# x^T k in column halves, relu on ScalarE for early k, mixing transposes behind the tokens', twelve z2 statistics on ScalarE

## Chip, cores and metric

The kernel runs on one core of one Trainium2 chip. The metric is the device time of one execution in microseconds (us): 251.74 us before, the median of three runs (251.51 to 251.84). A profiled execution took 250.06 us, of which 248.3 us lie between its first and its last instruction (the span). The granted TensorE clock was 0.999 of full speed.

## The reference

S = 2048 tokens, D = 512, all in bf16. A linear-attention block with 32 heads of 16 columns is followed by a gMLP block with F = 1792, Fh = 896:

```
h  = x + A(layernorm(x))
h2 = h + B(layernorm(h))

A(x): q, k, v = split(x @ wqkv)
      phi(t) = where(t > 0, t + 1, exp(t)) + 1e-06
      kv = einsum('bhsd,bhse->bhde', phi(k), v);  z = einsum('bhsd->bhd', phi(k))
      num = einsum('bhqd,bhde->bhqe', phi(q), kv)
      den = einsum('bhqd,bhd->bhq', phi(q), z)[..., None] + 1e-06
      return (num / den) @ wo
B(x): z = gelu(x @ w_in);  z1 = z[..., :Fh];  z2 = layernorm(z[..., Fh:])
      g = einsum('ts,bsf->btf', w_sp, z2) + b_sp[None, :, None]
      return (z1 * g) @ w_out
```

## The kernel before

Tokens are cut into 16 tiles of 128 (8 pairs, 4 groups of 512). Everything stays in SBUF (the on-chip working memory); PSUM, where TensorE writes, has 8 banks of 512 fp32 columns for each of 128 partitions. Five engines work side by side, each through its own instructions in order: TensorE (PE) multiplies, VectorE (DVE) and ScalarE (ACT) work element by element, GpSimd (POOL) does small vectors and issues some loads, SyncE (SP) issues most DMAs.

The stages:

1. Tiles of x are loaded and normalised. Statistics are on VectorE (`stats`, `aggr`, L610 and L614), the reciprocal root is Ln and Exp on ScalarE (L624, L626), and the scaling is on VectorE (L638) or, from tile 4 on for three tiles of each four, on ScalarE (L665).
2. Normalised tiles are transposed: tiles 0 to 3 by TensorE with a copy by ScalarE (L690, L695), the others by DMA transposes that SyncE issues (L679), one for each tile. L557 issues another kind of DMA transpose, for the mixing weights w_sp: 64 in all, 16 for each group of 512 output tokens (`wsp0` to `wsp3`).
3. The k projection of a token pair (`k_proj`, eight matmuls, L722) fills two PSUM banks, and so does the q projection of 512 tokens and 256 columns (`q_proj`, eight matmuls, L752). `phi` empties them: ScalarE takes Exp (L701) into an exp buffer `e`, VectorE takes the minimum with 1 (L702), and then the maximum of that and the PSUM tile plus 1 (L709). v is never formed. Instead x^T phi(k) is summed over all 16 tiles in four PSUM banks (`acc`, L739, four matmuls of 512 columns a tile); while it is open, two pairs of banks are left for k and q tiles.
4. x^T phi(k) is copied to SBUF in two row halves (L795 ScalarE, L797 VectorE), multiplied by w_v (L803), masked to the heads (L807), multiplied by w_o (L818) and copied (L823, L826) to give M. Column sums of phi(k) (L770, L774, L778, L787) give the denominators (`den`: L838, then Ln and Exp, L842 and L845), which are spread to all columns (L855 with copies L861, or L877) and scale phi(q) (L881).
5. For each unit of one or two tiles: h = x + phi(q) M (L910, L915), statistics, normalise to `hn` (L638; root on POOL, L631 and L633, but for the first tiles), transpose to `hT` (by TensorE for tiles 0 and 1, by DMA from SyncE's queue for the others).
6. z2 (L938, Gelu L947) by token tiles, with its layer norm, and z1 (L983, Gelu L988), transposed. The statistics of a z2 tile are two `bn_stats` and an aggregate on VectorE (L962) or, where `by_act` says so, a sum from the Gelu itself, a mean on POOL (L952), a Square with a sum on ScalarE (L954) and a division on POOL (L957).
7. Mixing: 16 matmuls for each of 28 tiles (L1013), bias and product on VectorE (L1019, L1022), then the output projection (L1031), the residual (L1037) and the store.

The order of each engine's queue is not that of the text. A planner (`Program.schedule`) runs before the instructions are emitted: each operation has an estimated cost, a priority and its dependencies, and the planner picks for each engine the operation that can start and has the lowest priority value. A list of numbers, `NUDGE`, one for each operation, is added to the priorities. So a change of a cost, of a priority or of the list moves instructions in all queues, and PSUM banks and buffers are handed out in the planned order. Semaphore waits follow from the planned order and the data.

Of the kernel before, what the change touches and what calls it, by code (L numbers as in the profile page):

```python
# [6 lines left out]
BF16 = mybir.dt.bfloat16  # L7
ACT = mybir.ActivationFunctionType
ALU = mybir.AluOpType
# [100 lines left out]
class Program:  # L110
# [294 lines left out]
def bass_sequential_preLN__linear_attn_block__mixer_gmlp__prompt_kernel(  # L405
# [41 lines left out]
    s_eb = Store(nc, "e", 3 * 2 * GW * 2)  # L447
# [55 lines left out]
    eb_v = View(s_eb, 0, [3, 2 * GW], BF16)  # L503
    EB = Pool(3, lambda s, w: eb_v.ap[:, s, :])
# [16 lines left out]
    def bank(i):  # L521
        return lambda a: a[:, i, :]

# [8 lines left out]
    def act_c(n, ps=True, ptr=0):  # L532
        return 0.15 + 0.00085 * n + 0.09 * ptr
# [20 lines left out]
    def load_wsp(tg, sts, after=()):  # L554
        for st in sts:
            dst = wsp[tg][st, :]
            op("sp", 1.3, lambda e, dst=dst, st=st: e.dma_start_transpose(  # L557
                dst.ap(), B_w_sp[tg * GW:(tg + 1) * GW, st * P:(st + 1) * P]),
               w=[dst], dma=(f"wsp{tg}", True), nbytes=-3 * P * GW * 2, prio=5000, after=after)

    load_wsp(0, range(NT))
    load_wsp(1, range(WSP1))


# [40 lines left out]
    op("pe", WARM * 2 * MM, spin, r=[warm], w=[acc()], prio=-9)  # L605
# [500 lines left out]
```

## Time and profile before

| what | number |
|---|---|
| median of three runs | 251.74 us |
| the profiled execution | 250.06 us |
| its span | 248.3 us |
| TensorE granted clock | 0.999 |
| TensorE busy, 0 to 10 / 10 to 20 us | 10.0 us long each: 6.74 / 8.08 |
| TensorE busy, 20 to 30 / 30 to 40 / 40 to 50 us | 9.64 / 9.71 / 9.66 |
| TensorE busy, 50 to 62 us | 10.70 of 12.00 |
| TensorE busy, 142 to 200 us | 57.74 of 58.00 |
| x^T k matmuls, L739 | 379 ns each with their drain, 64 of them issued |
| Exp in phi, L701 | 16 of 1025 ns |
| final of phi, L709 | 16 of 1223 ns |
| z2 statistics on ScalarE, L954 | 8 of 1042 ns, and 195 ns to read each sum |
| DMA transposes of w_sp, L557 | 2.8 us from issue to landing |

How to read it: the span is the time from the first to the last instruction on the chip; the profiled execution is one execution, so its time and the median differ. "Busy" is the time in which an engine has an instruction running. Matmuls overlap, so the mean duration of one (379 ns for 512 columns) is longer than the distance between two. A line number is that of the listing above; a helper's line (L610, L638, L690, L695, L679, L557) stands for several stages.

### The profile page before, as it was taken

To read this page: it belongs to the slowest core of one execution; us is meant where nothing else is said; L and a number is where in the kernel's file an instruction comes from. 1 tells how busy PE (TensorE), PEld (TensorE's weight loads), DVE (VectorE), ACT (ScalarE), POOL (GpSimd) and SP (SyncE) were. 2 spreads that over 40 slices of the span, in tenths; PEclk is the share of its full clock that TensorE was granted. 3 is DMA by queue.
4 is the path that set the end of the run, shared out by engine and by line. 5 is a ranking of instruction groups with operands and counts; after the bars stand their busy time and mean duration, and the time that the engine had idled before them with its cause. 6 is when DMAs were issued, how large, how long until landed. Compare 5 with 4: busy or idle time off the path is not lost.

```text
span 248.3 us, 2993 instructions
## 1 busy us (share of the span) xinstructions
PE 236.6 (95%) x1146; PEld 108.0 (43%) x1168; DVE 135.8 (55%) x256; ACT 81.9 (33%) x117; POOL 25.7 (10%) x66
## 2 busy tenths in 40 slices
PE   5699999997999999999999999999999999999995
PEld 1343444443444445454444444444444444444442
DVE  4997866559989999870233223343322523322443
ACT  3666674359944847978600300000000000000000
POOL 7100010110023332610200000000000000000000
PEclk9999999999999999999999999999999999999999
DMA  7985547899320340444744474111000110000022
GB/s 221 345 173 105 89 97 178 208 238 272 88 45 15 70 84 3 85 91 99 97 98 106 102 91 104 23 42 45 0 0 0 42 45 0 0 0 3 0 84 84
DMA packets 55870, 21.57 MB, mean 87 GB/s; under 512 B 49488, under 2 KB 55120, under 8 KB 55856
## 3 DMA queue, kind: packets, MB, share of 16 engines
q1 hardware_dynamic: 54928, 17.84, 32.6%
q0 software_dynamic: 656, 3.28, 4.2%
q10 hardware_dynamic: 272, 0.26, 0.3%
q8 instruction: 9, 0.15, 0.2%
q14 instruction: 5, 0.04, 0.1%
HBM read 7.47 MB, written 2.10 MB: 39 GB/s over the span
## 4 chain that ended last, share of the span: by engine, by line
PE 84%; DVE 6%; DMA 5%; ACT 2%; SPq 1%; issue 1%
PE ps L1013 39%; PE ps L983 10%; PE ps L938 10%; PE ps L1031 10%; PE ps L910 5%; PE ps L722 4%; PE ps L739 3%; DMA xT_pq_z<-pk_xn_z 3%; PE ps L752 2%; DMA xh<-in_A_x_dram 2%; DVE small L610 2%; ACT e L701 2%; DVE xT_pq_z L709 1%; DVE xT_pq_z L881 1%; SPq L540 1%
## 5 line engine op out<-in xcount | busy, mean ns | idle before, releaser
L1013 PE MATMUL ps<-wsp,pk_xn_z 128*128 128x512 bf16 x328 | 72.9, 379 | 0.4
L1019 DVE TENSOR_TENSOR r<-ps,e 128x512 bf16<-128x512 f32 x28 | 19.4, 692 | 68.2 <-PE ps L1013 68.2
L1013 PEld LDWEIGHTS ps<-wsp,pk_xn_z 128*128 128x128 bf16 x336 | 32.9, 98 | 39.6
L938 PE MATMUL ps<-win,hT 128*128 128x384 bf16 (+1 forms) x124 | 25.8, 352 | 0.6 <-issue 0.4
L983 PE MATMUL ps<-hT,win 128*128 128x512 bf16 x110 | 25.5, 379 | 0.1
L1031 PE MATMUL ps<-wout,xT_pq_z 128*128 128x512 bf16 x111 | 24.6, 379 | 0.1
L1013 PE MATMUL ps<-wqkv_wsp,pk_xn_z 128*128 128x512 bf16 x110 | 24.2, 379 | 0.1
L610 DVE BATCH_NORM_STATS2 small<-xh 128x6 f32<-128x512 bf16 x32 | 21.4, 677 | 3.8 <-DMA xh<-in_A_x_dram 3.5
L701 ACT ACTIVATE e<-ps 128x1024 bf16<-128x1024 f32 x16 | 16.4, 1025 | 18.7 <-PE ps L752 10.9
L988 ACT ACTIVATE xT_pq_z<-ps 128x1024 bf16<-128x1024 f32 x14 | 14.1, 1020 | 19.6 <-PE ps L983 19.5
L947 ACT ACTIVATE pk_xn_z<-ps 128x896 bf16<-128x896 f32 x16 | 14.6, 917 | 13.3 <-PE ps L938 12.6
L938 PEld LDWEIGHTS ps<-win,hT 128*128 128x128 bf16 x128 | 12.5, 98 | 13.1 <-DVE xh L915 0.7
L1037 DVE TENSOR_TENSOR r<-ps,xh 128x512 bf16<-128x512 f32 x16 | 11.1, 692 | 11.7 <-PE ps L1031 11.7
L1031 PEld LDWEIGHTS ps<-wout,xT_pq_z 128*128 128x128 bf16 x112 | 11.0, 98 | 13.2
L1013 PEld LDWEIGHTS ps<-wqkv_wsp,pk_xn_z 128*128 128x128 bf16 x112 | 10.9, 98 | 13.2
L722 PE MATMUL ps<-wqkv_wsp,xT_pq_z 128*128 128x512 bf16 x64 | 15.3, 379 | 1.4 <-DMA xT_pq_z<-pk_xn_z 1.4
L752 PE MATMUL ps<-xT_pq_z,wqkv_wsp 128*128 128x512 bf16 x64 | 15.1, 379 | 1.3 <-ACT xT_pq_z L695 1.3
L983 PEld LDWEIGHTS ps<-hT,win 128*128 128x128 bf16 x112 | 10.9, 98 | 12.6 <-DVE hn L638 0.2
L910 PE MATMUL ps<-pk_xn_z,xT_pq_z 128*128 128x512 bf16 x64 | 15.1, 379 | 0.4 <-DVE xh L915 0.3
L739 PE MATMUL ps<-pk_xn_z 128*128 128x512 bf16 x60 | 14.9, 379 | 0.2
L638 DVE TENSOR_SCALAR pk_xn_z<-pk_xn_z,small 128x896 bf16<-128x896 bf16 x16 | 7.3, 507 | 10.5 <-POOL small L633 10.5
L1022 DVE TENSOR_TENSOR xT_pq_z<-xT_pq_z,r 128x512 bf16<-128x512 bf16 x28 | 11.9, 425 | 1.0
(81 smaller groups left out, 182.0 us busy)
## 6 DMA issues: line engine op xcount, KB each, us to landing
out_dram<-r SPq DMA_DIRECT2D x16, 128.0 KB, 1.7
xh<-in_A_x_dram SPq DMA_DIRECT2D x7, 256.0 KB, 4.9
win<-in_B_w_in_dram POOLq DMA_DIRECT2D x1, 1792.0 KB, 8.2
wqkv_wsp<-in_A_wqkv_dram SPq DMA_DIRECT2D x2, 512.0 KB, 6.6
wout<-in_B_w_out_dram POOLq DMA_DIRECT2D x1, 896.0 KB, 6.6
wsp<-in_B_w_sp_dram SPq DMA_TRANSPOSE x48, 2.8
wqkv_wsp<-in_A_wo_dram POOLq DMA_DIRECT2D x1, 512.0 KB, 4.5
e<-in_B_b_sp_dram SPq DMA_DIRECT2D x1, 512.0 KB, 4.4
```

Source lines behind the costliest of these rows:

```text
L610: op("dve", dve_c(512), lambda e: e.bn_stats(s6.ap(), src.ap()), r=[src], w=[s6], prio=prio)
L701: op("act", act_c(1024), lambda e: e.activation(e_().ap(), t(flat).ap(), ACT.Exp), r=[t()], w=[e_()], prio=prio)
L722: i = e.matmul(t(bank(ti)).ap(), lhsT=lhs.ap()[:, c, :], rhs=rhs.ap()[:, c, :], start=(c == 0), stop=(c == KD - 1))
L739: i = e.matmul(acc(bank(c)).ap(), lhsT=l.ap()[:, c * P:(c + 1) * P], rhs=r_.ap(), start=(n == 0), stop=(n == NT - 1))
L752: r_ = e.matmul(t(bank(i)).ap(), lhsT=lhs.ap()[:, c, :], rhs=rhs.ap()[:, c, :], start=(c == 0), stop=(c == KD - 1))
L910: i = e.matmul(t(bank(ti)).ap(), lhsT=l.ap()[:, c, :], rhs=mw[c, :].ap(), start=(c == 0), stop=(c == KD - 1))
L938: k = e.matmul(t(bank(i)).ap()[:, 0:b - a], lhsT=l.ap()[:, c, :], rhs=win[c, a:b].ap(), start=(c == 0), stop=(c == KD - 1))
L947: op("act", act_c(FH, ptr=by_act), lambda e, t=t, d=d, acc={"accum_out": m.ap()} if by_act else {}: e.activation(d.ap(), t(flat).ap()[:, 0 ...
L983: k = e.matmul(t(bank(i)).ap(), lhsT=l.ap()[:, c, :], rhs=r_.ap()[:, c, :], start=(c == 0), stop=(c == KD - 1))
L1013: k = e.matmul(t(bank(0)).ap(), lhsT=l.ap()[:, s - a, :], rhs=r_.ap()[:, s - a, :], start=(s == 0), stop=(s == NT - 1))
L1019: op("dve", dve_c(512), lambda e: e.tensor_tensor(gb().ap(), t(bank(0)).ap(), bsp().ap()[:, tg * GW:(tg + 1) * GW], ALU.add), r=[t(), bsp( ...
L1031: k = e.matmul(t(bank(0)).ap(), lhsT=l.ap()[:, fc, :], rhs=wout[fc, :].ap(), start=(fc == 0), stop=(fc == KF - 1))
```

## The change

Eight things are changed together.

- **x^T k in halves.** Each tile's product is made of eight matmuls of 256 columns (`HW`) instead of four of 512. The four banks of `acc` are laid out anew: banks 0 and 1 hold the first 256 columns of phi(k) for all four row blocks, banks 2 and 3 the other 256. From pair `AS` = 5 on, the two halves are separate operations. The first matmul no longer opens the sum with `start`: the eight warm-up matmuls on zeros (`spin`), which all went to bank 0, go round the four banks, and the last four leave the sums open.
- **What follows x^T k** is split the same way: each half is copied by its own engine, multiplied by w_v (eight matmuls), and masked (256 columns).
- **Relu by ScalarE** for the k tiles of pairs 0 and 1 (`FR` = 2): `phi` copies relu(t) to a second exp buffer, and VectorE ends with a `tensor_tensor` add of two SBUF tiles in place of the `scalar_tensor_tensor` on PSUM. There are four exp buffers in place of three.
- **The mixing transposes** that SyncE issues early: five of `wsp0` ahead of the first token transposes (`WSP0` = 5); the other eleven and eight of `wsp1` (`WSP1`, was ten) wait until the token transposes have been issued.
- **z2 statistics:** `ZD` = 1 instead of 2, so 12 tiles of 16 take them on ScalarE instead of 8.
- Two of the planner's costs (1.3 to 1.31 for DMA transposes of one tile, and 0.76 for a normalise on ScalarE).
- A new list `NUDGE`, for the new number of operations. By it the order in all queues differs: among others, the statistics of tiles 0 and 1 are aggregated one by one, tiles 2 and 3 are transposed one by one, three q tiles and the column sums stand between the last halves of x^T k, w_in is loaded ahead of w_out, and the denominators of group 3 stand ahead of those of groups 1 and 2.
- `NA` = 1 is unchanged; `N0` = 4 only names a number that stood in the code.

```diff
-    WSP1 = 10
-    DB, DC, SPP, PK, ZD = 6, 7, 8, 0.3, 2
+    AS, FR, FQ, N0, WSP0 = 5, 2, 0, 4, 5
+    WSP1 = 8
+    DB, DC, SPP, PK, ZD = 6, 7, 8, 0.3, 1
...
+    def half(tile, h, fn=None):
+        o = tile(fn)
+        o.keys = [tile.keys[0] + (i,) for i in ((0, 1) if h is None else (h,))]
+        return o
...
-    load_wsp(0, range(NT))
-    load_wsp(1, range(WSP1))
+    load_wsp(0, range(WSP0))
...
+    HW = GW // 2
+    def xk(h, c):
+        return lambda v: v[:, 2 * h + c // 2, c % 2 * HW:(c % 2 + 1) * HW]
     def spin(e):
-        for _ in range(WARM):
-            i = e.matmul(acc(bank(0)).ap(), lhsT=warm.ap()[:, 0:P], rhs=warm.ap(), start=True, stop=True)
+        for w in range(WARM):
+            i = e.matmul(acc(bank(w % KD)).ap(), lhsT=warm.ap()[:, 0:P], rhs=warm.ap(), start=True, stop=w < WARM - KD)
         return i
...
-    def phi(t, dst, prio, two=False):
+    def phi(t, dst, prio, two=False, relu=False):
         e_ = Tile(EB)
         op("act", act_c(1024), lambda e: e.activation(e_().ap(), t(flat).ap(), ACT.Exp), r=[t()], w=[e_()], prio=prio)
+        if relu:
+            u = Tile(EB)
+            op("act", act_c(1024), lambda e: e.activation(u().ap(), t(flat).ap(), ACT.Relu), r=[t()], w=[u()], prio=prio)
...
+            if relu:
+                return e.tensor_tensor(d, a, b, ALU.add)
+            return e.scalar_tensor_tensor(d, a, 1.0 + EPS_PHI, b, op0=ALU.add, op1=ALU.max)
...
-        for n in (2 * p, 2 * p + 1):
-            l, r_ = xn[n, :], pk[n, :]
-            def mm(e, n=n, l=l, r_=r_):
-                for c in range(KD):
-                    i = e.matmul(acc(bank(c)).ap(), lhsT=l.ap()[:, c * P:(c + 1) * P], rhs=r_.ap(), start=(n == 0),
-                                 stop=(n == NT - 1))
-                return i
-            op("pe", 4 * MM, mm, r=[l, r_], w=[acc()], prio=10 * p + KA)
+        for h in ((None,) if p < AS else (0, 1)):
+            for n in (2 * p, 2 * p + 1):
+                hs = (0, 1) if h is None else (h,)
+                l, r_ = xn[n, :], pk[n, hs[0] * HW:(hs[-1] + 1) * HW]
+                def mm(e, n=n, l=l, hs=hs):
+                    for g_ in hs:
+                        for c in range(KD):
+                            i = e.matmul(acc(xk(g_, c)).ap(), lhsT=l.ap()[:, c * P:(c + 1) * P],
+                                         rhs=pk.ap[:, n, g_ * HW:(g_ + 1) * HW], start=False,
+                                         stop=(n == NT - 1 and c % 2 == 1))
+                    return i
+                op("pe", 2 * MM * len(hs), mm, r=[l, r_], w=[half(acc, h)], prio=10 * p + KA + 9 * (h or 0))
...
+    load_wsp(0, range(WSP0, NT), by_dma_ops)
+    load_wsp(1, range(WSP1), by_dma_ops)
...
+    kvmT = [Tile(XN), Tile(XN)]
     for h in range(2):
-        d = xtk[2 * h:2 * h + 2, :]
-        s = acc(lambda v, h=h: v[:, 2 * h:2 * h + 2, :])
+        a, z = h * GW // 2, (h + 1) * GW // 2
+        d = xtk[:, a:z]
+        s = half(acc, h, lambda v, h=h: v[:, 2 * h:2 * h + 2, :].rearrange("p b (t f) -> p (b t) f", t=2))
...
+        vk, m = Tile(PS), kvmT[h]
+        def mm(e, h=h, vk=vk):
+            for i in range(2):
+                c = 2 * h + i
+                for j in range(KD):
+                    k = e.matmul(vk(bank(0)).ap()[:, i * P:(i + 1) * P], lhsT=wv.ap[:, j, c * P:(c + 1) * P],
+                                 rhs=xtk.ap[:, j, c * P:(c + 1) * P], start=(j == 0), stop=(j == KD - 1))
+            return k
+        op("pe", 8 * 0.058, mm, r=[wv.all(), d], w=[vk()], prio=Q0 + 2)
+        op("dve", 0.4, lambda e, vk=vk, m=m: e.tensor_tensor(
+            m().ap()[:, 0:2 * P].rearrange("p (c f) -> p c f", c=2),
+            vk(bank(0)).ap()[:, 0:2 * P].rearrange("p (c f) -> p c f", c=2),
+            bmask.ap.rearrange("p (a f) -> p a f", a=1).to_broadcast([P, 2, P]), ALU.mult),
+           r=[vk(), bmask.all()], w=[m()], prio=Q0 + 2)
```

In the changed program L764 is the line of the x^T k matmuls, L719 that of relu, L744 and L778 those of the k and q projections, L826 and L828 the copies of the halves.

More of the change, by code (lines that the diff above doesn't have):

```diff
@@ L652, in bass_sequential_preLN__linear_attn_block__mixer_gmlp__prompt_kernel @@
         rstd_of(st_x[grp[0]:grp[-1] + 1, 7], rs.all(), pr)
-        by_act = [n for n in grp if n >= 4 and n % 4 >= NA]
+        by_act = [n for n in grp if n % 4 >= NA and n >= N0]
         if by_act:
@@ L697, in transpose_pair @@
                r=[t()], w=[d], prio=prio + 1)
-    def phi(t, dst, prio, two=False):
+    def phi(t, dst, prio, two=False, relu=False):
         e_ = Tile(EB)
         op("act", act_c(1024), lambda e: e.activation(e_().ap(), t(flat).ap(), ACT.Exp), r=[t()], w=[e_()], prio=prio)
+        if relu:
+            u = Tile(EB)
+            op("act", act_c(1024), lambda e: e.activation(u().ap(), t(flat).ap(), ACT.Relu), r=[t()], w=[u()], prio=prio)
         op("dve", 0.12 + 0.27, lambda e: e.tensor_scalar(e_().ap(), e_().ap(), 1.0, EPS_PHI, op0=ALU.min, op1=ALU.add),
            r=[e_()], w=[e_()], prio=prio)
+        x_ = u if relu else t
         def fin(e):
-            a, b = t(None if two else flat).ap(), e_().ap()
+            a, b = (u() if relu else t(None if two else flat)).ap(), e_().ap()
             if two:
                 b = b.rearrange("p (a b) -> p a b", a=2)
-            return e.scalar_tensor_tensor(dst.ap() if two else flat(dst.ap()), a, 1.0 + EPS_PHI, b, op0=ALU.add,
-                                          op1=ALU.max)
-        return op("dve", dve_c(1024), fin, r=[t(), e_()], w=[dst], prio=prio)
+                a = a.rearrange("p (a b) -> p a b", a=2) if relu else a
+            d = dst.ap() if two else flat(dst.ap())
+            if relu:
+                return e.tensor_tensor(d, a, b, ALU.add)
+            return e.scalar_tensor_tensor(d, a, 1.0 + EPS_PHI, b, op0=ALU.add, op1=ALU.max)
+        return op("dve", dve_c(1024, mode=2 if relu else 1), fin, r=[x_(), e_()], w=[dst], prio=prio)
     def k_proj(p, wt, prio):
@@ L730, in bass_sequential_preLN__linear_attn_block__mixer_gmlp__prompt_kernel @@
         t = k_proj(p, wk, 10 * p)
[L731 removed]
+        o = phi(t, pk[2 * p:2 * p + 2, :], 10 * p, relu=p < FR)
         if p == 6:
             load("pool", "win", win.all(), B_w_in.rearrange("(c p) f -> p c f", p=P), D * F * 2, after=[o])
[L734 to L742 removed]
+        for h in ((None,) if p < AS else (0, 1)):
[10 more added lines that the diff above has]
+                op("pe", 2 * MM * len(hs), mm, r=[l, r_], w=[half(acc, h)], prio=10 * p + KA + 9 * (h or 0))
     def q_proj(gq, f, prio):
@@ L755, in q_proj @@
             op("pe", 4 * MM, mm, r=[lhs, rhs], w=[t()], prio=prio)
-        return phi(t, pqT[f:f + 2, gq * GW:(gq + 1) * GW], prio, two=True)
+        return phi(t, pqT[f:f + 2, gq * GW:(gq + 1) * GW], prio, two=True, relu=gq < FQ)
+    load_wsp(0, range(WSP0, NT), by_dma_ops)
+    load_wsp(1, range(WSP1), by_dma_ops)
     Q0 = 10 * NP
@@ L797, in bass_sequential_preLN__linear_attn_block__mixer_gmlp__prompt_kernel @@
             op("dve", dve_c(1024), lambda e, d=d, s=s: e.tensor_copy(d.ap(), s.ap()), r=[s], w=[d], prio=Q0 + 2)
-    vk, kvmT = Tile(PS), Tile(XN)
-    def mm(e):
-        for c in range(KD):
-            for j in range(KD):
-                i = e.matmul(vk(bank(0)).ap()[:, c * P:(c + 1) * P], lhsT=wv.ap[:, j, c * P:(c + 1) * P],
-                             rhs=xtk.ap[:, j, c * P:(c + 1) * P], start=(j == 0), stop=(j == KD - 1))
-        return i
-    op("pe", 16 * 0.058, mm, r=[wv.all(), xtk.all()], w=[vk()], prio=Q0 + 2)
-    op("dve", dve_c(512), lambda e: e.tensor_tensor(
-        kvmT().ap().rearrange("p (c f) -> p c f", c=KD), vk(bank(0)).ap().rearrange("p (c f) -> p c f", c=KD),
-        bmask.ap.rearrange("p (a f) -> p a f", a=1).to_broadcast([P, KD, P]), ALU.mult),
-       r=[vk(), bmask.all()], w=[kvmT()], prio=Q0 + 2)
+        vk, m = Tile(PS), kvmT[h]
[12 more added lines that the diff above has]
+           r=[vk(), bmask.all()], w=[m()], prio=Q0 + 2)
     for b in range(2):
@@ L818, in bass_sequential_preLN__linear_attn_block__mixer_gmlp__prompt_kernel @@
             op("pe", MM, lambda e, t=t, i=i, c=c, r_=r_: e.matmul(
-                t(bank(i)).ap(), lhsT=kvmT().ap()[:, c * P:(c + 1) * P], rhs=r_.ap(), start=True, stop=True),
-               r=[kvmT(), r_], w=[t()], prio=Q0 + 3.5)
+                t(bank(i)).ap(), lhsT=kvmT[c // 2]().ap()[:, c % 2 * P:(c % 2 + 1) * P], rhs=r_.ap(), start=True,
+                stop=True), r=[kvmT[c // 2](), r_], w=[t()], prio=Q0 + 3.5)
         d = mw[2 * b:2 * b + 2, :]
```

15 lines of the change are left out of this document (7 added, 8 removed), and 57 rows, old and new, of the table NUDGE.

## The prediction

> **What bounds the kernel now.** I read the first part of the page (busy time), then the chain that ended last, then TensorE's timeline over the first 62 us, then SyncE's queue over the same stretch, and last the busy times by stage.
>
> ```profile
> span 248.3 us, 2993 instructions
> PE 236.6 (95%) x1146; PEld 108.0 (43%) x1168; DVE 135.8 (55%) x256; ACT 81.9 (33%) x117; POOL 25.7 (10%) x66
> ...
> PE 84%; DVE 6%; DMA 5%; ACT 2%; SPq 1%; issue 1%
> ```
>
> TensorE carries the span; a gain must come out of its idle time. In the chain, from 61.23 us to 245.40 us it never leaves TensorE but for "issue" pieces of 0.05 us and one of 0.41 us. So nearly all the idle time lies before 61.23 us. TensorE's timeline (start, busy, what, idle before):
>
> ```profile
> 14.79 1.89 PE L739 MATMUL ps<-pk_xn_z 128*128 128x512 bf16 x7
> 16.52 1.89 PE L752 MATMUL ps<-xT_pq_z,wqkv_wsp 128*128 128x512 bf16 x8
> 19.00 1.02 PE L722 MATMUL ps<-wqkv_wsp,xT_pq_z 128*128 128x512 bf16 x4 [0.59 <-DMA xT_pq_z<-pk_xn_z]
> 20.23 1.04 PE L722 MATMUL ps<-wqkv_wsp,xT_pq_z 128*128 128x512 bf16 x4 [0.20 <-DMA xT_pq_z<-pk_xn_z]
> ...
> 30.24 1.89 PE L722 MATMUL ps<-wqkv_wsp,xT_pq_z 128*128 128x512 bf16 x8 [0.34 <-DMA xT_pq_z<-pk_xn_z]
> ...
> 41.04 1.89 PE L722 MATMUL ps<-wqkv_wsp,xT_pq_z 128*128 128x512 bf16 x8 [0.28 <-DMA xT_pq_z<-pk_xn_z]
> ...
> 52.47 1.90 PE L752 MATMUL ps<-xT_pq_z,wqkv_wsp 128*128 128x512 bf16 x8
> 54.21 0.24 PE L778 MATMUL ps<-small,hn 128*128 128x2 bf16 x4
> ...
> 61.23 1.04 PE L910 MATMUL ps<-pk_xn_z,xT_pq_z 128*128 128x512 bf16 x4 [0.30 <-DVE xh L915]
> ```
>
> Eight 512-column matmuls start 1.73 us after the eight before (14.79, 16.52), 0.216 us each; the 1.89 shown includes the drain. Counted by starts, k tile 4 stands 0.75 us late (16.52 + 1.73 = 18.25, start 19.00), tile 5 0.37, the fifth k pair 0.50, the seventh 0.44. All four wait for a DMA transpose of normalised x. Why they are late is in SyncE's queue:
>
> ```profile
> 7.29 9.01 SPq L557 DMA_TRANSPOSE wsp<-in_B_w_sp_dram  x6
> 16.34 5.19 SPq L679 DMA_TRANSPOSE xT_pq_z<-pk_xn_z  x4
> 21.57 4.69 SPq L557 DMA_TRANSPOSE wsp<-in_B_w_sp_dram  x3
> 26.31 5.19 SPq L679 DMA_TRANSPOSE xT_pq_z<-pk_xn_z  x4
> 31.55 5.18 SPq L557 DMA_TRANSPOSE wsp<-in_B_w_sp_dram  x4
> ```
>
> Token tile 4 was normalised by 13.3 us (VectorE, L638, 12.87 for 0.40) but issued at 16.34, behind six mixing-weight transposes of 1.50 us each (9.01 / 6).
>
> **The change, part by part.** The order of each queue is that of the changed program.
>
> *Mixing transposes behind the tokens'.* Five instead of six stand before tile 4, none between the token groups; 12 follow tile 15, then the bias load, 7 more, then the h transposes. Tile 4 is issued at 7.29 + 5 x 1.50 = 14.8 and, with the old 2.66 us from issue to use (16.34 to 19.00), usable at 17.5. Tile 5, one 1.30 us issue later, at 18.73, where it was 20.23: 1.50 us. For the others I walked the queues. Tile 9 is ready when ScalarE has normalised it (about 22.0), tile 8 when VectorE has (about 23.4); landing 2.6 later at 24.7 and 26.1, they are due at 28.2. Tiles 12 to 15 land by 37.9 and are due from 36.9 on, the last at 39.9. So the 0.50 and 0.44 go too. Sum: 2.44.
>
> Does something else stop TensorE first? Each q or k tile fills two of four free banks, and its phi must empty them. Rows of one k tile: last matmul issued by 24.56, Exp 24.75 to 25.78, min/add 25.81, final at 26.27 for 1.22, banks free 2.95 us after the tile. The tile after next starts two blocks later, 3.46 us. In the new order this spacing holds at every tile, with 0.4 to 0.5 us of slack, as before. I count 0.
>
> *LayerNorm statistics one by one.* Tile 0's transposes can start at about 5.0 instead of 6.12, but then TensorE waits for tile 5 anyway: 0.
>
> *x^T k in halves.* 64 matmuls of 512 columns become 128 of 256, with 64 more weight loads. No such stream is in the trace. Bounds: 512 columns take 0.216, 384 take 0.162 (L938, 1.51 for four of each), 128 take 0.055 (L690, four in 0.22) to 0.059 (L803, 16 in 0.94), every one with its own load. 256 then take 0.108 to 0.113: 128 of them 13.8 to 14.4 against 13.8. I take 13.8, as the loads (98 ns) fit inside 108, and keep +0.6. The Trainium skill (TensorE: Matmul & The Clock Gate, Back-to-back issue gap) says that in a stream of load and matmul pairs the load counts too, some 81 ns at 128 columns instead of 56; an estimate by that, 25 ns on each of 128, would add 3.2 us. L803's 59 ns disagrees with it.
>
> What the halves gain: the last half's sum ends the stretch, with the three last q tiles and the column sums before it. The old stretch ended with q at 54.21. The new one ends at T = 54.21 - 2.44 - 0.09 (a gap at 51.40 that the new order fills) = 51.68. From there the way to the continuous stream is again a VectorE queue: final of the last q phi (it started when its Exp was done) to T + 1.15, zc 0.15, masked halves 0.4 each around 0.6 of waiting for ScalarE's half copy and eight matmuls, 0.8 until the M matmuls are done, cast 1.15, three scalings 0.6 + 1.15 + 0.6: T + 7.0 to 7.3. Before, 61.23 - 54.21 = 7.02. Cost 0.2; the halves save a wait, but the same VectorE casts and scalings stand behind it. Bounds: -1.0 (if half of the 2.15 us idle there goes: 7.02 less matmuls of 4.87: L778 0.1, L803 0.94, L838 0.98, L818 0.86, L877 0.87, four of L910 0.86, L855 0.25) to +0.6.
>
> *Tile 0 of h.* Its first z2 matmul now follows a second spread and a y pair. Residual add, statistics, Ln, Exp, normalise, transpose, copy (0.69 + 0.70 + 0.18 + 0.5 + 0.4 + 0.4 + 0.6) run through queues with four more spread copies of 1.02 on ScalarE; I find 1.07 us of TensorE idle there, where before has 0.1 + 0.41: cost 0.5. Bounds 0 and 1.
>
> *Relu.* Two more PSUM passes on ScalarE at about 10 and 16 us. Relu isn't in the trace; Exp of that shape is 1.025, Copy 1.019. VectorE saves 2 x (1.22 - 0.68), the second being L881's all-SBUF form. Hidden behind TensorE's wait for tile 5; without that cover 2 us on ScalarE delay two phis by 1. I take 0.
>
> *Twelve statistics on ScalarE.* Four tiles move: ScalarE + 4 x (1.04 + 0.20 + 0.20) = 5.8, POOL + 4 x (0.26 + 0.37), VectorE - 4 x (0.67 + 0.55 + 0.21) = 5.7. The stages:
>
> ```profile
> 62.00:82.00 20.00, 19.49 (x104) 9.17 (x103) 18.99 (x38) 11.63 (x20) 3.77 (x8) 1.00 0.23 53
> 82.00:102.00 20.00, 19.90 (x103) 9.91 (x102) 18.78 (x45) 14.89 (x23) 7.77 (x17) 1.00 0.24 49
> 102.00:122.00 20.00, 19.89 (x97) 9.39 (x97) 8.62 (x22) 15.99 (x25) 5.76 (x13) 1.00 0.54 100
> ```
>
> Columns after the length: PE, PEld, DVE, ACT, POOL. ScalarE has 17.5 us idle here, VectorE 2.2 in the first 40 us, so the load moves to the emptier engine. Walking bank by bank, TensorE finds its banks free with 0.5 us or more at each z1 and z2 tile: 0. Behind a Square that waits for POOL's mean (0.35 to 0.54 each) stand the Gelus that free banks.
>
> *Queues passed.* w_in is loaded before w_out, right after pair 6's phi (about 42, was 50.74), so the first z2 has it. On SP, 12 transposes from 36.7 end at 54.5, the bias load (waiting for the last phi, 52.9) and 7 more end at 65.6; the first h transpose is due at 68.9: covered by 3.3 us. A fourth exp buffer costs nothing.
>
> **Sum:** -1.50 - 0.50 - 0.44 - 0.09 + 0.2 + 0.5 = -1.83. The profiled execution took 250.06, 1.76 beyond its span; less 1.83 it gives 248.2. It stands 1.68 below the median of 251.74, so the median becomes 249.9.
>
> **Rivals.**
> 1. More: the transition shortens by the 1.0 of its bound. For it: the copy of the first half lies under matmuls. Against: VectorE's queue. 248.9.
> 2. Part is eaten: phi's slack of 0.4 to 0.5 is missing at two or three tiles, or z tiles wait for banks, in all 1.1. For it: many tight hops, relu ahead of ScalarE's normalises. Against: the same spacing held before without a stall. 251.0.
> 3. No change: the mixing transposes that were pushed back hold up the h transposes. They issue at 1.30 to 1.56 us; from 1.66 each (19 in 31.6) the first h is late, and at 1.75 the gain is gone. 251.7.
> 4. Slower: ScalarE's in-order queue in the z stage. Each moved tile costs it 1.44 and about 0.45 of waiting for POOL, 7.6 in all; if a third (2.5) shows as TensorE waiting for banks, 249.9 + 2.5 = 252.4. It decides from 1.83 on. Against: 17.5 us idle.
> 5. Slower: the extra weight loads don't hide. 64 x 0.098 = 6.3 at worst; from 29 ns each the gain is gone. At 0.05 each 253.1. By the skill's pair rule the kernel would be slower too; the 59 ns row speaks against both.
>
> **How the numbers follow.** Forecast 0.50, rival 1 0.14, rival 2 0.16, rival 3 0.06, rival 4 0.11, rival 5 0.03. Faster (by over 0.2%, 0.5 us, about what this measurement can tell) 0.50 + 0.14 + 0.16 = 0.80; same 0.06; slower 0.14. Range 248.5 (rival 1 with 0.4 less) to 251.8 (rivals 2 and 3); outside lie rivals 4 and 5 and a little below. The forecast alone: 249.2 to 250.6.
>
> **What would show it.** Right: SyncE issues tile 4's transpose near 14.8; no k tile after 20 us waits over 0.1 for a DMA; the last x^T k starts near 50.8; L764's spacing is 0.108; the stream is continuous from 59; the z stage keeps TensorE at 19.5 of 20. Wrong: waits of q or k tiles on VectorE or ScalarE between 20 and 50, or of z tiles on Gelu or Square between 70 and 120.

## The result, and the profile after

The changed kernel took 248.67 us (median of 13 runs, 247.32 to 251.03) beside 251.10 us for the kernel before on the same chip (13 runs, 249.84 to 251.84): a ratio of 0.9897, 95% interval 0.987 to 0.9924, which is 2.6 us less (the 251.03 is a run in the chip's slower state and not in the ratio; the medians as they stand are 2.43 apart). The forecast was 249.9 us, a gain of 1.83. The profiled execution of the changed kernel took 249.17 us with a span of 247.2.

The spans of its 13 runs are not evenly spread: four lie between 245.4 and 245.7 us, the others between 246.6 and 247.9 but for the one of 251.03 (249.3). This will matter below.

The busy times and the chain that ended last, from the page of the changed kernel:

```profile
span 247.2 us, 3128 instructions
PE 238.0 (96%) x1208; PEld 115.3 (47%) x1232; DVE 130.0 (53%) x245; ACT 88.6 (36%) x131; POOL 26.6 (11%) x74
...
PE 91%; ACT 3%; DVE 2%; DMA 2%; issue 1%; SPq 0%
```

VectorE's share of the chain fell from 6% to 2%, DMA's from 5% to 2%. TensorE was busy for 1.4 us more (238.0 against 236.6), about as much as the slow first k pair shown below cost, while the span is 1.1 shorter: what was won is idle time. TensorE's timeline of the changed kernel (start, busy, what, idle before):

```profile
1.37 3.60 PE L618 MATMUL ps<-small 128*128 128x512 bf16 x8 [1.37 <-POOL small L575]
...
7.24 3.45 PE L744 MATMUL ps<-wqkv_wsp,xT_pq_z 128*128 128x512 bf16 x8
...
12.72 1.90 PE L778 MATMUL ps<-xT_pq_z,wqkv_wsp 128*128 128x512 bf16 x8 [1.58 <-ACT xT_pq_z L710]
...
21.38 1.91 PE L764 MATMUL ps<-pk_xn_z 128*128 128x256 bf16 x16
23.13 1.89 PE L744 MATMUL ps<-wqkv_wsp,xT_pq_z 128*128 128x512 bf16 x7
...
53.69 0.24 PE L807 MATMUL ps<-small,hn 128*128 128x2 bf16 x4
...
59.86 2.76 PE L943 MATMUL ps<-pk_xn_z,xT_pq_z 128*128 128x512 bf16 x12
62.83 0.40 PE L888 MATMUL ps<-r,sel 32*128 32x512 bf16 x4 [0.20 <-ACT r L878]
...
65.97 1.69 PE L971 MATMUL ps<-win,hT 128*128 128x512 bf16 x8 [0.30 <-ACT hT L710]
```

The same two places of the kernel before:

```profile
7.36 1.94 PE L722 MATMUL ps<-wqkv_wsp,xT_pq_z 128*128 128x512 bf16 x8
...
11.33 1.90 PE L752 MATMUL ps<-xT_pq_z,wqkv_wsp 128*128 128x512 bf16 x8 [1.28 <-ACT xT_pq_z L695]
```

Three things are to be seen. No k or q tile waits for a DMA transpose any more. The first k pair (L744 at 7.24) takes 3.45 us for eight matmuls that took 1.94 before: this execution began at half pace, and its first q tile starts at 12.72, 1.39 later than before (11.33), so the profiled gain is smaller than the timed one. And from the end of the x^T k stretch (L807, 53.69) to the start of the continuous stream (L943, 59.86) it takes 6.17 us, where it took 7.02 (54.21 to 61.23). SyncE's queue in the same run:

```profile
7.76 7.64 SPq L567 DMA_TRANSPOSE wsp<-in_B_w_sp_dram  x5
15.45 23.02 SPq L694 DMA_TRANSPOSE xT_pq_z<-pk_xn_z  x12
38.50 19.97 SPq L567 DMA_TRANSPOSE wsp<-in_B_w_sp_dram  x12
...
59.14 9.45 SPq L567 DMA_TRANSPOSE wsp<-in_B_w_sp_dram  x7
```

Five mixing transposes, then all twelve of the tokens in one row, then the rest. The last ends at 68.59, and the h transposes are issued from 69.88 on. The busy times by stage (length, PE, PEld, DVE, ACT, POOL) for the z stage:

```profile
62.00:82.00 20.00, 19.28 (x103) 9.11 (x104) 19.44 (x38) 15.33 (x25) 4.68 (x11) 1.00 0.39 70
82.00:102.00 20.00, 19.90 (x100) 9.85 (x101) 11.88 (x29) 15.25 (x27) 6.88 (x20) 1.00 0.27 53
```

ScalarE has 3.7 us more in the first of them, VectorE 6.9 less in the second, and TensorE is as busy as it was to within 0.2 us.

### The profile page after: what moved, and what is told of

It reads as the page before. It is cut to its first block, busy times and chain, and to the rows that moved or that the text cites. A ratio compares the mean times of both kernels' runs of the same rounds, so it can differ in the third digit from the quotient of the medians.

```text
span 247.2 us, 3128 instructions
## 1 busy us (share of the span) xinstructions
PE 238.0 (96%) x1208; PEld 115.3 (47%) x1232; DVE 130.0 (53%) x245; ACT 88.6 (36%) x131; POOL 26.6 (11%) x74
## 4 chain that ended last, share of the span: by engine, by line
PE 91%; ACT 3%; DVE 2%; DMA 2%; issue 1%; SPq 0%
PE ps L1046 39%; PE ps L1016 10%; PE ps L971 10%; PE ps L1064 10%; PE ps L778 6%; PE ps L744 5%; PE ps L764 5%; PE ps L943 5%; DMA xh<-in_A_x_dram 2%; ACT e L716 1%; ACT wqkv_wsp L894 1%; DVE xT_pq_z L732 0%; PE ps L705 0%; PE ps L910 0%; ACT wqkv_wsp L826 0%
## 5 line engine op out<-in xcount | busy, mean ns | idle before, releaser
L971 PE MATMUL ps<-win,hT 128*128 128x512 bf16 (+1 forms) x127 | 26.6, 352 | 0.3 <-ACT hT L710 0.3
L1016 PE MATMUL ps<-hT,win 128*128 128x512 bf16 x109 | 26.0, 379 | 0.3
L1070 DVE TENSOR_TENSOR r<-ps,xh 128x512 bf16<-128x512 f32 x16 | 11.1, 691 | 11.7 <-PE ps L1064 10.9
L1064 PEld LDWEIGHTS ps<-wout,xT_pq_z 128*128 128x128 bf16 x112 | 10.9, 98 | 13.2
L1046 PEld LDWEIGHTS ps<-wqkv_wsp,pk_xn_z 128*128 128x128 bf16 x112 | 10.9, 98 | 13.2
L1016 PEld LDWEIGHTS ps<-hT,win 128*128 128x128 bf16 x112 | 10.9, 98 | 12.6
L778 PE MATMUL ps<-xT_pq_z,wqkv_wsp 128*128 128x512 bf16 x63 | 15.1, 379 | 1.6 <-ACT xT_pq_z L710 1.6
L744 PE MATMUL ps<-wqkv_wsp,xT_pq_z 128*128 128x512 bf16 x60 | 16.3, 410 | 0.2
L764 PE MATMUL ps<-pk_xn_z 128*128 128x256 bf16 x128 | 15.9, 273 | 0.0
L943 PE MATMUL ps<-pk_xn_z,xT_pq_z 128*128 128x512 bf16 x62 | 14.7, 379 | 0.2 <-issue 0.2
L764 PEld LDWEIGHTS ps<-pk_xn_z 128*128 128x128 bf16 x128 | 12.4, 98 | 4.2 <-issue 0.4
```

Of the source, the lines that this page charges most:

```text
L744: i = e.matmul(t(bank(ti)).ap(), lhsT=lhs.ap()[:, c, :], rhs=rhs.ap()[:, c, :], start=(c == 0), stop=(c == KD - 1))
L764: i = e.matmul(acc(xk(g_, c)).ap(), lhsT=l.ap()[:, c * P:(c + 1) * P], rhs=pk.ap[:, n, g_ * HW:(g_ + 1) * HW], start=False, stop=(n == NT ...
L778: r_ = e.matmul(t(bank(i)).ap(), lhsT=lhs.ap()[:, c, :], rhs=rhs.ap()[:, c, :], start=(c == 0), stop=(c == KD - 1))
L943: i = e.matmul(t(bank(ti)).ap(), lhsT=l.ap()[:, c, :], rhs=mw[c, :].ap(), start=(c == 0), stop=(c == KD - 1))
L971: k = e.matmul(t(bank(i)).ap()[:, 0:b - a], lhsT=l.ap()[:, c, :], rhs=win[c, a:b].ap(), start=(c == 0), stop=(c == KD - 1))
L1016: k = e.matmul(t(bank(i)).ap(), lhsT=l.ap()[:, c, :], rhs=r_.ap()[:, c, :], start=(c == 0), stop=(c == KD - 1))
```

## The experiments

Each timed kernel was compared with runs of the kernel before on the same chip; chips differ by some tenths of a us, so ratios are compared where two kernels ran on different ones. It helps to cut each profiled span in four, all read from TensorE's timeline: when the first q tile starts, from there to T (the end of the last x^T k or q matmuls, where L778 of before or L807 of the changed kernel starts), from T to the continuous stream (the transition), and from there to the end.

| kernel | first q | q to T | transition | rest | span |
|---|---|---|---|---|---|
| before | 11.33 | 42.88 | 7.02 | 187.07 | 248.3 |
| changed | 12.72 | 40.97 | 6.17 | 187.34 | 247.2 |
| before, SyncE's queue of the change | 13.78 | 41.30 | 7.01 | 187.11 | 249.2 |
| changed, SyncE's old queue | 12.72 | 49.21 | 6.18 | 187.29 | 255.4 |
| changed, halves joined | 10.91 | 42.25 | 7.09 | 187.35 | 247.6 |
| changed, 14 warm-ups | 12.19 | 40.97 | 6.17 | 187.37 | 246.7 |
| before, 14 warm-ups | 11.45 | 43.17 | 7.01 | 187.07 | 248.7 |
| changed, no relu | 12.48 | 42.39 | 6.17 | 187.36 | 248.4 |
| changed, 4 tiles' statistics back | 10.85 | 41.62 | 6.17 | 187.76 | 246.4 |
| changed, 11 warm-ups | 10.59 | 41.27 | 6.17 | 187.27 | 245.3 |
| before, 11 warm-ups | 11.91 | 43.01 | 7.03 | 187.05 | 249.0 |
| before, SyncE's queue, 11 | 11.64 | 41.30 | 7.02 | 187.04 | 247.0 |
| changed, no relu, 11 | 11.15 | 42.38 | 6.18 | 187.29 | 247.0 |
| changed, joined, 11 | 10.78 | 42.15 | 7.09 | 187.28 | 247.3 |

Each row is one execution. The transition and the rest repeat to about 0.1 us between kernels that share a part (the one with four tiles' statistics back differs by its edit). Most of the noise is in the first column, and some of it comes back in the second: where the first q tile is early, TensorE reaches a token tile that has not landed and waits for it (changed: 40.97 from a start at 12.72, 41.27 from one at 10.59).

**SyncE's queue alone, in the kernel before.** After planning, SyncE's queue is put in the changed order (`w` mixing transposes, `t` the tokens', `b` bias, `h` those of h):

```diff
+        new = ld + w[:5] + t + w[5:17] + b + w[17:24] + h + w[24:] + st
...
+        self.order["sp"] = new
```

> The kernel before, with SyncE's queue alone reordered to that of the change: 5 mixing transposes, then all 12 token transposes, then 12 mixing ones, the bias load, 7 more, the h transposes, the rest. All other queues stay. Theory A (the gain comes from token transposes that no longer wait behind mixing transposes): tile 4's transpose issued near 15, the waits of k tiles on DMA (0.75, 0.37, 0.50, 0.44 us before) go, 1.5 to 2.1 us faster than before, ratio 0.992 to 0.994. Rival B (the gain comes from the split of x^T k and what follows it, and the earlier tiles only wait elsewhere): ratio 0.998 to 1.001.

Measured: 250.47 us, ratio 0.9959 (0.9936 to 0.9983). The interval touches what either theory expected, so the timing alone doesn't decide. The trace does: q to T fell from 42.88 to 41.30, and of the four DMA waits one is left, that of the seventh k pair:

```profile
41.91 1.89 PE L739 MATMUL ps<-wqkv_wsp,xT_pq_z 128*128 128x512 bf16 x8 [0.33 <-DMA xT_pq_z<-pk_xn_z]
```

(The late first q tile of this execution has two causes: x came late, VectorE had to wait for a tile of it until 6.14, so that TensorE stood idle for 2.64 us after its warm-ups; and the first k pair then ran at half pace, 3.06 us for eight.)

**SyncE's old queue in the changed kernel.**

```diff
+        new = ld + w[:6] + t[:4] + w[6:9] + t[4:8] + w[9:13] + t[8:] + w[13:17] + b + w[17:24] + h + w[24:] + st
...
+        self.order["sp"] = new
```

> The changed kernel with SyncE's queue alone put back: 6 mixing transposes, 4 token ones, 3, 4, 4, 4, then 4 mixing ones, the bias load, 7, the h transposes and the rest. Theory A: the k tiles wait for their transposes again, 1.5 to 2.4 us of the 2.6 us gain are lost, ratio to before 0.996 to 1.000. Rival B: little is lost, ratio 0.989 to 0.992.

Measured: 257.59 us, ratio 1.0227 (1.0197 to 1.0258), by the ratios 8.3 us slower than the changed kernel, far more than either theory had. All of it lies between first q and T. TensorE's timeline of this kernel around the loss:

```profile
41.13 3.42 PE L761 MATMUL ps<-wqkv_wsp,xT_pq_z 128*128 128x512 bf16 x8 [2.24 <-DMA xT_pq_z<-pk_xn_z]
...
48.51 1.03 PE L761 MATMUL ps<-wqkv_wsp,xT_pq_z 128*128 128x512 bf16 x2 [2.50 <-DMA xT_pq_z<-pk_xn_z]
```

and its busy times behind the first wait (after the length PE, PEld, DVE, ACT, POOL, the granted clock, the DMA share, GB/s):

```profile
42.00:46.00 4.00, 4.00 (x14) 1.52 (x12) 0.35 (x1) 1.02 (x1) 0.00 (x0) 0.66 0.88 331
```

The last four token transposes are issued from 36.46 to 41.67, where the changed kernel has them from 33.3 on (tiles 12 to 15). The first lands after 4.5 us, beside the load of w_o, and TensorE waits 2.24 us for it. It then runs the next eight matmuls at half pace (3.42 us instead of 1.89). The fourth is issued at 40.4, beside the load of w_in (1792 KB, issued by POOL at 40.26; in the kernel before that load came at 50.74, behind all token transposes). It lands after 8.1 us (median 2.5), and TensorE waits another 2.50 us. That the load of w_in makes this landing long is read from their times; no run moved the load alone. As it stands, the changed order of the other engines needs the changed queue of SyncE: the two parts can't be priced one by one from the changed side.

**Halves joined.** Both multiplications by w_v wait for both half copies, so that the half that is copied last is again the only one that counts:

```diff
+        for o in self.vk:
+            for c in self.cp:
+                o.deps[c] = True
+                o.raw.add(c)
```

> The changed kernel in which both multiplications by w_v wait for the copies of both halves, so that splitting x^T k saves no wait (the matmuls stay 256 columns wide, the queues stay). Theory A with the transition as the profile of the changed kernel has it (6.2 us from the last x^T k to the continuous stream, 7.0 before): 0.6 to 0.9 us slower than the changed kernel, ratio to before 0.992 to 0.994. Rival B: most of 2.6 us lost, ratio 0.997 to 1.000. My prediction's sum, in which the halves save nothing: no loss, 0.989 to 0.991.

Measured: 250.11 us, ratio 0.9933 (0.9906 to 0.9959): 0.9 us given back, as theory A had it, though the interval reaches into that of the changed kernel (0.987 to 0.9924). In the table the transition returns to 7.09. The same with 11 warm-ups:

> The changed kernel in which both multiplications of the halves with w_v wait for both half copies of the sums, with 11 warm-up multiplications. Theory A (the halves shorten the transition from the last sum to the next full run of TensorE, 6.17 us against 7.09): 0.7 to 1.0 us slower than the changed kernel with 11, ratio 0.987 to 0.988. The prediction's view (the halves save nothing, as the same VectorE work stands behind them): within 0.3 us, ratio 0.983 to 0.985.

Measured: 249.10 us, ratio 0.9919 (0.9893 to 0.9944), against 0.984 for the changed kernel with 11: 2.0 us, more than either theory. Its timeline, and from VectorE's the cast of M:

```profile
23.23 1.04 PE L754 MATMUL ps<-wqkv_wsp,xT_pq_z 128*128 128x512 bf16 x4 [0.61 <-DMA xT_pq_z<-pk_xn_z]
...
54.26 0.61 PE L846 MATMUL ps<-wqkv_wsp 128*128 128x128 bf16 x8 [1.08 <-DVE zc L826]
...
56.22 1.23 DVE L870 CAST pk_xn_z<-ps 128x1024 bf16<-128x1024 f32 x1
```

The second line is the edit: 0.92 us in the transition. (The row names zc, which was done by 53.7; what ended just before 54.26 is ScalarE's half copy, at 54.15.) The cast of M starts 3.29 us after T (52.93), as late as in the kernel before (3.33). The first line is not the edit's doing: token tile 7's transpose, issued at 19.0, landed after 4.1 us instead of 2.5, and q to T grew by 0.88. That longer landing is in three of the profiled runs (both joined kernels, and the one without relu and with 11), and what causes it stays open. So the halves are worth 0.85 to 0.92 us by the traces; the larger timed difference is not all theirs.

**Warm-ups.** The changed kernel with 14 multiplications on zeros ahead of the work instead of 8, and with 11:

```diff
-        for w in range(WARM):
...
+        for w in range(14):
...
```

> The changed kernel with 14 warm-up matmuls instead of 8. In its profile the first k tiles ran at half pace (eight matmuls in 3.25 us), in the profile of before at full pace (1.73). Theory C (each execution starts at half pace until TensorE has been busy long enough, and 8 warm-up matmuls are now and then too few): with 14 the first k tile runs at 0.216 us a matmul in every execution, the upper cluster of times (span 246.6 to 247.9) goes to the lower (245.4 to 245.7), 0.8 to 1.5 us faster than the changed kernel, ratio 0.983 to 0.987. Rival D (the longer warm-up only delays the first transposes, which start at 5.7): up to 1 us slower or no change, ratio 0.989 to 0.994.

Measured: 248.13 us (247.68 to 248.83), ratio 0.9857 (0.9831 to 0.9883).

> The changed kernel with 11 warm-up multiplications, between its own number and 14. Theory C: 14 held TensorE at full pace but put the first transposes off to 7.19 us; 11 ends about 1.3 us earlier. If 11 are enough, the same as with 14 or up to 0.5 us better, ratio 0.983 to 0.986, and runs close together. If they are not, the runs fall into two clusters some 1.5 us apart as the changed kernel's do, ratio 0.987 to 0.991.

Measured: 247.53 us (247.07 to 248.45), ratio 0.984 (0.9815 to 0.9866), the fastest kernel of this study: 4.2 us under the median of the kernel before on its chip. The timeline with 11:

```profile
1.37 3.94 PE L618 MATMUL ps<-small 128*128 128x512 bf16 x11 [1.37 <-POOL small L575]
5.15 0.39 PE L705 MATMUL ps<-small,pk_xn_z 128*128 128x128 bf16 x4
...
6.67 1.89 PE L744 MATMUL ps<-wqkv_wsp,xT_pq_z 128*128 128x512 bf16 x8
...
10.59 1.90 PE L778 MATMUL ps<-xT_pq_z,wqkv_wsp 128*128 128x512 bf16 x8 [1.47 <-ACT xT_pq_z L710]
...
51.86 0.24 PE L807 MATMUL ps<-small,hn 128*128 128x2 bf16 x4
...
58.03 2.76 PE L943 MATMUL ps<-pk_xn_z,xT_pq_z 128*128 128x512 bf16 x12
```

The eleventh ends at 5.31, hardly later than the eighth did (4.97), because the last ones already ran at full pace in this execution; then the first k pair takes 1.89 us. The span, 245.3, is that of the changed kernel's four shortest runs (245.4 to 245.7). So its two groups of runs fit starts at full and at half pace; the kernels with eight warm-ups that were profiled from a full-pace start (halves joined, four tiles' statistics back) have their first q tile near 10.9 as well. With 14 the work itself can be held up: in that profile they took 5.98 us, at half pace nearly to the end, and the first transposes start at 7.19.

Is that gain the changed kernel's alone?

> The kernel before with 14 warm-up multiplications instead of its own number. Theory C (TensorE often starts the token transposes at half pace, and a longer warm-up takes that away for either kernel): the profiled execution of before had started at full pace and lay 1.0 to 1.7 us under its median, so the median falls to 249.5 to 250.3 us, ratio 0.994 to 0.997, and the runs lie closer together. Rival D (the gain of the longer warm-up belongs to the changed kernel's order alone, because before waits for DMA transposes of x at its k tiles anyway and loses the gain there): ratio 0.998 to 1.004.

Measured: 250.68 us (250.2 to 250.83), ratio 0.9958 (0.9942 to 0.9973): theory C. The longer warm-up helps the kernel before as well, and from 14 warm-ups each the change is still worth 1.0% (0.9857 against 0.9958).

> The kernel before with 11 warm-up multiplications: the start alone, so that the parts of the change can be compared from one start. Theory C: as with 14, or up to 0.5 us better, ratio 0.993 to 0.996, with runs close together. Against the changed kernel with 11 (ratio 0.984) the whole change would then be worth 2.3 to 3.0 us from one and the same start. Rival D2 (a good part of the change's gain was a luckier start): ratio 0.987 to 0.991, so that less than 1.7 us is left for the change.

Measured: 251.07 us, ratio 0.9995 (0.9978 to 1.0011): neither. The kernel before gets nothing from 11. Its profiled run did start at full pace, but its first two groups of transposes start at 6.64 and 7.71, where the first profile of before has 6.12 and 7.12: VectorE had to wait until 5.53 for a tile of x (5.05 there). Whether 11 are too few in most runs of this kernel, or x was late on that chip, stays open. From 11 each the change looks larger, 0.984 against 0.9995, and by the open point this is not only its doing.

**SyncE's queue in the kernel before, with 11 warm-ups.**

> The kernel before with only SyncE's queue in the changed order (the mixing transposes behind the tokens'), with 11 warm-up multiplications. Theory A: as without them, 1.0 to 1.7 us better than the kernel before with 11, so ratio 0.987 to 0.991: the waits of 0.65, 0.17 and 0.75 us for DMA transposes of x are gone. Rival (tile 5's transpose is late by its normalisation and not by the queue, so its wait stays): 0.5 to 0.9 us better, ratio 0.990 to 0.993.

Measured: 249.36 us, ratio 0.9943 (0.9918 to 0.9968), on one chip with the 251.07 above: medians 1.7 us apart, as theory A had it (its ratio is missed because the kernel before gained nothing from 11). Eight of its twelve runs lie between 248.75 and 249.70, four between 250.85 and 251.40; what sets the four apart is open. q to T fell from 43.01 to 41.30, that is 1.71 us, where the changed kernel with 11 has 41.27. So SyncE's queue alone brings this stretch to where the changed kernel has it, though the two are not made up alike: here the seventh k pair still waits 0.33 us for its transpose, and the changed kernel, whose first q tile is 1.05 earlier, waits 0.3 us for tile 5 instead.

**No relu on ScalarE.** The last step of phi reads PSUM on VectorE again, and the two relu passes are taken out of ScalarE's finished queue; all else keeps its order:

```diff
-            if relu:
-                return e.tensor_tensor(d, a, b, ALU.add)
             return e.scalar_tensor_tensor(d, a, 1.0 + EPS_PHI, b, op0=ALU.add, op1=ALU.max)
```

> The changed kernel without the two passes of relu on ScalarE: the last step of phi of the early k reads the sums in PSUM on VectorE as in the kernel before; every other order is kept. The prediction put the relu at nothing: 248.2 to 249.2 us. Theory R (a relu of 1 us ahead of tile 7's normalisation on ScalarE makes its transpose late): 0.5 to 0.8 us faster where TensorE starts at full pace, nothing where it starts at half pace, so a ratio of 0.987 to 0.990 and tile 7's normalisation about 1 us earlier in the trace. Rival: slower by 0.3 to 1.0 us, because VectorE gets back some 1.1 us of work ahead of tiles 6 and 7: ratio 0.991 to 0.995.

Measured: 249.76 us, ratio 0.9925 (0.9896 to 0.9954), 0.7 us slower: the rival's range. The interval touches that of the changed kernel, but theory R's 0.987 to 0.990 is all but outside it, and q to T is 1.42 longer. With 11 warm-ups, on another chip:

> The changed kernel without the relu passes on ScalarE, with 11 warm-up multiplications. Theory V (the relu takes 0.5 us off VectorE in each early phi, and VectorE is late with phi there): 0.6 to 1.1 us slower than the changed kernel with 11, ratio 0.9865 to 0.9885, with a wait for VectorE's phi at the third k tile. Theory R (from a full-pace start the relu holds up tile 7's normalisation on ScalarE): equal or up to 0.5 us faster, ratio 0.982 to 0.984.

Measured: 248.79 us, ratio 0.9907 (0.9887 to 0.9928), 1.7 us slower than the changed kernel with 11 (0.9815 to 0.9866), and here the intervals are apart. Its timeline has two waits that the changed kernel has not:

```profile
13.28 1.04 PE L766 MATMUL ps<-wqkv_wsp,xT_pq_z 128*128 128x512 bf16 x4 [0.23 <-DVE pk_xn_z L751]
...
19.49 1.90 PE L766 MATMUL ps<-wqkv_wsp,xT_pq_z 128*128 128x512 bf16 x8 [0.84 <-DVE pk_xn_z L751]
```

A k tile needs PSUM banks that VectorE still reads for an earlier phi (L751). The first of these reads ends at 13.23 (12.02 for 1.21) and the matmuls start at 13.28. In the changed kernel with 11, which started 0.56 us earlier, ScalarE's relu has read that tile by 11.45 (10.42 for 1.03), and the add that is left on VectorE takes 0.68 us instead of 1.21. By the table relu is worth 1.1 us of q to T from 11 warm-ups (42.38 against 41.27, of which the second holds the 0.3 of waiting for tile 5) and 1.4 from eight (42.39 against 40.97); what else the timed 1.7 holds (its first q tile is 0.56 later) was not parted.

**Four tiles' z2 statistics back on VectorE.**

```diff
+                if n % 4 < 2:
+                    bn = []
...
+                        bn.append((lambda e, s6=s6, src=src: e.bn_stats(s6.ap(), src.ap()), 0.6))
...
+                    g.zst.append((go, pm, so, pd, bn))
```

(Shown is only where the statistics on VectorE are made; they replace those on POOL and ScalarE in the finished queues, so that nothing else moves.)

> The changed kernel with the z2 statistics of the four tiles that the change moved to ScalarE back on VectorE (each two half statistics of 0.6 us and a small aggregate), all else in the same order. Prediction (moving them costs and gains nothing): within 0.3 us of the changed kernel, ratio 0.9885 to 0.991. Rival Z (VectorE is over 95% busy from 62 to 82 us and is what sets the pace there): 1 to 3 us slower, ratio 0.994 to 1.002. Rival 4 of the prediction (the statistics on ScalarE delay the gelu of later tiles): faster by 0.5 to 0.7 us, ratio 0.987 to 0.988.

Measured: 248.40 us, ratio 0.988 (0.9851 to 0.991): the interval holds the changed kernel's 0.9897 and rival 4's 0.987 to 0.988, and rival Z (0.994 and more) is out. In the one trace the rest is 187.76 us, 0.4 to 0.5 above the changed kernels' 187.27 to 187.37. TensorE falls behind the changed kernel with 11 at three places: by 0.1 us near 80.6, and by 0.2 each near 85.5 and 92.2. So in the new order ScalarE's statistics are worth 0.4 to 0.5 us by this trace; the timing can't tell it from nothing.

## Why the prediction was right, and where it was not

The 248.67 us lie inside the range (248.5 to 251.8), but below what the forecast alone allowed (249.2 to 250.6) and close to rival 1's 248.9.

- **What bounds the kernel, and the mixing transposes: right in the sum, not in its parts.** The four DMA waits were the gain to be had in the first part. Tile 5 usable at 18.73, T at 51.68 was the forecast; with 11 warm-ups, from a full-pace start like that of the profile it was worked out from, T is 51.86. SyncE's queue alone takes 1.6 to 1.7 us from q to T, and the earlier first q tile (10.59 instead of 11.33) the other 0.7. The prediction gave all of it to SyncE's queue: its 1.50 for tile 5 is more than the two waits it counted there (0.75 + 0.37 = 1.12). The other 0.38 can only be had if TensorE comes to tile 5 earlier than before, and the step that brings this it put at 0 (statistics, below). In the changed kernel's own profiled run T is 53.69, because it began at half pace. The prediction read one execution of before that had begun at full pace and took this start for given; it carried the difference to the median (1.68 us) over as a constant. In the changed kernel the four short runs took 247.32 to 247.54 us and the median is some 1.2 above them; that this came near 1.68 is luck, as nothing in the prediction worked it out.
- **The transition: the term that failed.** "Cost 0.2; the halves save a wait, but the same VectorE casts and scalings stand behind it." It measured -0.85, near the bound of -1.0: rival 1's mechanism is what happened. VectorE's queue in the changed kernel shows why:

```profile
53.09 1.23 DVE L732 SCALAR_TENSOR_TENSOR xT_pq_z<-ps,e 128x1024 bf16<-128x1024 f32 x1
54.23 0.20 DVE L816 TENSOR_TENSOR zc<-small,ps 128x32 bf16<-128x32 bf16 x1
54.43 0.42 DVE L839 TENSOR_TENSOR hn<-ps,small 128x256 bf16<-128x256 f32 x1
55.62 0.42 DVE L839 TENSOR_TENSOR hn<-ps,small 128x256 bf16<-128x256 f32 x1 [0.77 <-PE ps L835]
56.05 1.22 DVE L859 CAST pk_xn_z<-ps 128x1024 bf16<-128x1024 f32 x1
```

  The last final of phi is done by T + 0.54 (54.23, where zc starts) and not by T + 1.15. And the cast of M (L859) follows the second mask at once, at T + 2.36: the matmuls it needs come from the half that was ready first and ran while VectorE waited for the other and masked it. I had put 0.8 us for those matmuls behind the second mask, and the cast at T + 3.5. The casts and scalings are the same, they start 1.1 us sooner. With the halves joined the cast is back at T + 3.29, so it is the wait for both halves that is saved, and not the queue's new order.
- **256-column matmuls, 0 (bounds 0 to +0.6): right.** Sixteen of L764 start 1.75 us before what follows them (21.38 to 23.13), 0.109 us each; 128 make 14.0 against 13.8. (One of the rows it rests on was read a little high: L803's sixteen take 1.05 us with the last one's 0.22, so they start 0.055 apart and not 0.059; the bounds hardly move.) The Trainium skill's figure for pairs of load and matmul (TensorE: Matmul & The Clock Gate, Back-to-back issue gap), which would have made the kernel slower, is not what this stream shows.
- **Tile 0 of h, +0.5: too high.** TensorE has two idle pieces there (0.20 and 0.30, where before has 0.41; a third of 0.16, shown as "issue", is a matmul missing from this trace: with 11 warm-ups eight are there and no gap), and the rest grew by 0.20 to 0.30 only.
- **Relu, 0: right as a part of the new order, wrong as a price.** That no phi stalls in the new order was forecast and held; the reason given (ScalarE's extra work is hidden) missed that without relu VectorE holds the banks for too long. It is worth 1.1 to 1.4 us there.
- **Twelve statistics, 0: held as a part of the new order.** Rival 4's loss is not seen: TensorE is 19.28 and 19.90 of 20 us busy in the z stage. By one trace the new order with the four tiles back on VectorE would be 0.4 to 0.5 us longer, a price that the prediction put at nothing.
- **SyncE's other passes, 0: held, with less to spare than thought.** TensorE waits for no h transpose. But the twelve mixing transposes behind the tokens' took 1.66 us each (19.97 / 12) where the prediction's 36.7 to 54.5 makes 1.48, and the queue was done 1.29 us before the first h transpose (68.59, 69.88) and not 3.3.
- **Statistics of tiles 0 and 1 one by one, 0: mis-sized.** The first transposes do start at 5.06 to 5.15 in five executions with the changed order, as forecast (about 5.0), and later where the warm-ups were longer or x came later. "Then TensorE waits for tile 5 anyway" is true of 0.3 us only: with 11 warm-ups the first q tile is 0.7 us earlier than in the first profile of before. The five changed kernels that were profiled from a full-pace start with 8 or 11 warm-ups have it at 10.59 to 11.15, the four kernels with the old order of the start at 11.33 to 11.91. No run changes these statistics alone, so how much of the earlier start is theirs is not shown.

With 11 warm-ups against the profile of before the four columns give -0.74 - 1.61 - 0.85 + 0.20 = -3.00 us, where the prediction had -1.83; the transition makes 1.05 of the 1.17 between them. (This sets 11 warm-ups against eight; both executions started at full pace.) The earlier start, the growth of the rest, the planner's two costs and the order of w_in and w_out were not parted by any run.

## What to carry to other kernels

When a product is split so that a first part is ready early, work out which later instruction needs only that part and where it then stands in its engine's queue: the halves were worth 0.9 us here because a cast stood right there in VectorE's queue, with its matmuls already done. Queue orders of different engines belong together: putting one back (SyncE's) cost 8.3 us, three times what the whole change had brought. And look at how a run starts before two profiles are compared: here a start at half pace hid 1.5 us or more of the gain in the changed kernel's own profile.

## What the runs showed of the hardware

- TensorE starts at half pace: in both kernels' own profiles the eight warm-ups take 3.60 us, about 0.43 each and a drain. After them it went on at full pace in some executions (L722 x8 in 1.94 us) and at half pace in others (L744 x8 in 3.45). When full pace comes differs from run to run: 11 warm-ups took from 3.94 us (some four of them at full pace) to 4.88 (none), 14 took 4.60 in one run and 5.98 in another. Worked out from 0.43 and 0.216 us each, that is between 2.8 and 5.6 us after the first matmul; in the changed kernel's own profile, where gaps of 0.76 and 0.51 us follow the eight warm-ups, it was some 9 us (the first k pair, up to 10.5, is still slow). The Trainium skill (TensorE: Matmul & The Clock Gate, Part 1: The HAM clock gate) gives some 3.4 us of activity, counted in time and not in matmuls; this lies inside the spread, but a warm-up made for 3.4 us is too short for many of these runs. The recorded granted clock is no sure witness: it is 1.00 from 5 to 10.5 us in the changed run that was at half pace there, though in the run of before with SyncE's queue changed it reads 0.50 from 8 to 11 us.
- A wait of 2.24 us was enough to bring TensorE back to half pace (changed kernel with SyncE's old queue: 3.42 us for eight matmuls; granted clock 0.66 from 42 to 46 us). So was one of 2.64 us after the warm-ups (before with SyncE's queue changed: the first four transposes behind it still take 0.40 us, the next four, after another 0.58 us of idle, 0.61).
- Most DMA transposes of a token tile (128 x 512) land 2.4 to 2.8 us after their issue. Those issued while the load of w_o (512 KB; from 33.63 in the changed kernel) is under way land later, the slowest of each run after 3.7 to 4.9, and one beside that of w_in (1792 KB) after 8.1. Tile 7's took 4.1 in three runs with no such load beside it.
